# Pairing the leftover attention tiles of neighbouring head pairs, with another order of tiles, normalizations and turns of k and q

## The chip, the cores and the metric

The kernel runs on one NeuronCore of a Trainium2 chip. The metric is the device time of one execution in microseconds (us), the median of five runs. Engines are named as the profile names them: PE (matrix multiply; PEld is its weight load), DVE (vector engine), ACT (activation engine), POOL (GpSimd), SP (the queue from which nearly all DMAs are issued). L12 means line 12 of the kernel.

## The reference

Attention with a threshold on 8 batches of 8 heads (576 positions, head size 64), then a two-layer network with the activation h - tanh(h) on the 4608 x 512 result:

```python
scores = scale * np.matmul(q, k.transpose(0, 1, 3, 2))
thresh = np.max(scores, axis=-1, keepdims=True) - tau
scores = np.where(scores >= thresh, scores, -1000000000.0)
scores = scores - np.max(scores, axis=-1, keepdims=True)
attn = np.exp(scores)
attn = attn / (np.sum(attn, axis=-1, keepdims=True) + 1e-09)
attn_out = np.matmul(attn, v)
...
x = attn_out.transpose(0, 2, 1, 3).reshape(B * S, H * D)   # B*S = 4608, H*D = 512
h = x @ w_in                                               # d_ff = 2048
out = (h - np.tanh(h)) @ w_out
```

## The kernel before

**Tiles.** The 64 heads are taken in 32 pairs p. A head has 576 query rows: four tiles of 128 rows, and 64 rows over. The 64 rows over of the two heads of a pair make one *shared* tile. So a pair has nine tiles (TPP = 9), 288 in all, numbered i = 9p + j. Before the change j = 0 to 3 are the first head, j = 4 is the shared tile, j = 5 to 8 the second head.

**Duos.** The four tiles of a head go in two *duos*: kinds "A" (j = 0, 2, 5, 7) and "B" (the tile after it). A duo's two score tiles are thresholded into one buffer z of 2 x 576 = 1152 columns, which is 9 blocks of 128; it is transposed, exponentiated and multiplied with v together. Where the 9 blocks are cut, the middle block holds the last 64 columns of the A tile beside the first 64 of the B tile; v is therefore kept with two half-empty chunks (4 and 5 of vb), one for each half. The shared tile is alone (kind "M"): its 576 columns stand in a buffer zm with 64 columns of padding, 5 blocks.

**The main loop** goes over steps s from -8 to about 292. One step issues, in this order, for different tiles:

- shift(s+7): the threshold bias nb of a duo (or of an M tile) on DVE, L354
- scores(s+8): PE matmuls of q against k in two fp16 parts, kT and kS, into a psS buffer of the pool ps_big (2 buffers), L327, or L317 for the shared tile; then on DVE the scaled copy with row maximum, L337
- kink(s+5): ACT writes z, L374; after the second tile of a duo (or an M tile) a DMA transpose z to zT on SP's queue, L382. The first six pairs transpose on PE instead (psZ, L394)
- weights(s): ACT's exp of zT into pT, L411 (L403 for the first six pairs)
- the network's work, about one piece in a step: four matmuls 128x512, of psH (L495) or of psY (L521), with tanh on ACT (L508) and h - tanh(h) on DVE (L514), and the copy yo of a finished psY (L534)
- attend(s-2): at the second tile of a duo, ten matmuls of pT and vb into psO (L440); for the shared tile five (L429)
- norm: DVE divides psO by its last column (L454, L455, for the shared rows L460), at j = 4 and j = 8; emit_x of the pair before at j = 1: PE transposes (L472, L478) and two DVE copies (L485, L486)
- what plan holds for this step: DMA loads of k, q and v, the split of k and q in two fp16 parts and of v on POOL (L190 to L194, L222 to L227), and turn

In the first four pairs weights and attend run four steps ahead of these numbers.

**turn(p, "k")** makes pair p's kT: nine PE transposes into a ps_big buffer (L241), a DVE copy (L264), then two POOL copies with the head halves swapped, kS (L270). turn(p, "q") makes qT in the same way without a swap; for odd p from 8 on, and p = 30, it is one DMA transpose instead (L253). Both stand at a distance before first = 9p - 8, the step that issues pair p's first scores: k at first - 5, q at first - 3 (by DMA first - 5). For p = 1 they are nearer.

Each engine works through its instructions in the order in which the loop issued them. The network's 32 pieces for a batch (four pairs, 36 steps) begin at the fifth step of the next batch, and are through when its 36 steps end; so at the first four steps of each batch (s = 36b to 36b + 3) PE has attention work alone. The text calls these four steps the *gap*. After step 292 only the network's last pieces are left (the *tail*).

To speak of places in the new order, r is the number of the step within two pairs: r = s mod 18, from 0 to 17, where the first pair is even.

Of the kernel before, what the change touches and what calls it, by code (L numbers as in the profile page):

```python
# [18 lines left out]
def kernel(  # L19
# [11 lines left out]
    nc = tc.nc  # L31
    P = 128
# [14 lines left out]
    NPAIR = B * HPAIR  # L47
    DM_C = d_model // P
    DF_C = d_ff // P
    TPP = 9  # L50
    NTILE = NPAIR * TPP

# [32 lines left out]
    NV = 4  # L85
    vbs = []
    for i in range(NV):
# [3 lines left out]
        nc.gpsimd.memset(vb[0:64, :, 4, D : D + 1], 1.0)  # L91
        nc.gpsimd.memset(vb[64:P, :, 5, D : D + 1], 1.0)
        vbs.append(vb)

    NM = 2
    zms = []
    for i in range(NM):
        zm = const.tile([P, 5 * P], BF16, name=f"zm{i}")
        nc.vector.memset(zm[:, S : 5 * P], -STEEP)
        zms.append(zm)  # L100

    mx3 = []
# [140 lines left out]
    def q_by_dma(p):  # L245

        return p >= 2 * HPAIR and (p % 2 == 1 or p == 30)
# [48 lines left out]
    REM = (slice(512, 576), slice(576, 640))  # L296
    scs, mxs, nbs, zs, zts, pts, ops = {}, {}, {}, {}, {}, {}, {}

    def kind(j):

        return "M" if j == 4 else "A" if j in (0, 2, 5, 7) else "B"

    def scores(i):
        p, j = divmod(i, TPP)
        qT, kT, kS = mats[p, "q"], mats[p, "k"], mats[p, "ks"]
        ps = ps_big.tile([P, 1024], F32, name="psS", tag="big")
        main, rem, lo = slice(0, 512), slice(512, 576), 0
        if kind(j) == "B":
            main, rem, lo = slice(512, 1024), slice(448, 512), 448
        if j == 4:  # L310
            qrem = REM
            if q_by_dma(p):
                qrem = (slice(512, 640, 2), slice(513, 640, 2))
            for n, kk in enumerate((kT, kS)):
                for dst, srcs in ((main, MAIN), (rem, REM)):
                    for hh in range(2):
                        nc.tensor.matmul(  # L317
                            out=ps[64 * hh : 64 * hh + 64, dst],
                            lhsT=qT[:, qrem[hh]], rhs=kk[:, srcs[hh]],
                            start=(n == 0), stop=(n == 1),  # L320
                        )
        else:
            hh = int(j > 4)
            lhs = qT[:, j * P : (j + 1) * P]
            for n, kk in enumerate((kT, kS)):
                for dst, src in ((main, MAIN[hh]), (rem, REM[hh])):
                    nc.tensor.matmul(  # L327
                        out=ps[:, dst], lhsT=lhs, rhs=kk[:, src],
                        start=(n == 0), stop=(n == 1),
                    )  # L330
        sc = sc_pool.tile([P, S], F32, name="sc")
        if kind(j) == "B":
            mx = mxs[i] = mxs.pop(i - 1)
        else:
            mx = mxs[i] = mx3[i // 2 % len(mx3)]
        c = int(kind(j) == "B")
        nc.vector.tensor_scalar(  # L337
            out=sc, in0=ps[:, lo : lo + S], scalar1=SC, scalar2=None,
            op0=ALU.mult, op1=ALU.max, accum_out=mx[:, c : c + 1],
        )  # L340
        scs[i] = sc

    def shift(i):

        kd = kind(i % TPP)
        if kd == "A":
            return
        mx = mxs.pop(i)
        nb = st_pool.tile([P, 9], F32, name="nb", tag="nb")
        o, m = nb[:, 0:1], mx[:, 0:1]  # L350
        if kd == "B":
            o = nb.rearrange("p (a b) -> p a b", b=3)[:, :, 0:2]
            m = mx.rearrange("p (a b) -> p a b", b=4)[:, :, 0:3]
        nc.vector.tensor_scalar(  # L354
            out=o, in0=m, scalar1=-1.0, scalar2=tau, op0=ALU.mult, op1=ALU.add
        )
        if kd == "B":
            nbs[i - 1], nbs[i] = nb[:, 0:1], nb[:, 1:2]
        else:
            nbs[i] = nb[:, 0:1]  # L360

    def kink(i):
        sc, nb = scs.pop(i), nbs.pop(i)
        kd = kind(i % TPP)
        if kd == "B":
            zt = zs.pop(i - 1)
            z = zt[:, S:W]
        elif kd == "A":
            zt = zs[i] = z_pool.tile([P, W], BF16, name="z")
            z = zt[:, 0:S]  # L370
        else:
            zt = zms[i // TPP % NM]
            z = zt[:, 0:S]
        nc.scalar.activation(  # L374
            out=z, in_=sc, func=ACT.Prelu, bias=nb, scale=1.0, alpha=STEEP
        )
        if on_pe(i):
            zts[i] = zt
        elif kd != "A":
            n = 5 if kd == "M" else TPP  # L380
            zts[i] = zt_pool.tile([P, TPP, P], BF16, name="zT")
            nc.sync.dma_start_transpose(out=zts[i][:, 0:n, :], in_=zt)  # L382

    def weights(i):


        kd = kind(i % TPP)
        n, off = {"A": (4, 0), "M": (5, 0), "B": (5, 4)}[kd]
        if on_pe(i):
            z = zts.pop(i)  # L390
            pl, tag = (ps_h, "h") if i % 2 and i < HPAIR * TPP else (ps_y, "y")
            ps = pl.tile([P, 5 * P], BF16, name="psZ", tag=tag)
            for c in range(n):
                nc.tensor.matmul(  # L394
                    out=ps[:, c * P : (c + 1) * P],
                    lhsT=z[:, (off + c) * P : (off + c + 1) * P],
                    rhs=ident_bf, is_transpose=True, start=True, stop=True,
                )
            if kd == "B":
                pt = pts.pop(i - 1)  # L400
            else:
                pt = p_pool.tile([P, TPP * P], FP16, name="pT")
            nc.scalar.activation(  # L403
                out=pt[:, off * P : (off + n) * P], in_=ps[:, 0 : n * P], func=ACT.Exp
            )
        elif kd == "A":
            return
        else:
            n += off
            pt = p_pool.tile([P, TPP * P], FP16, name="pT")  # L410
            nc.scalar.activation(  # L411
                out=pt[:, 0 : n * P], in_=zts.pop(i)[:, 0:n, :], func=ACT.Exp
            )
        pts[i] = pt

    def attend(i):

        p, j = divmod(i, TPP)
        kd, vb = kind(j), vbs[p % NV]
        if kd == "A":  # L420
            return
        if j in (1, 6):
            ops[p, int(j > 4)] = ps_o.tile([P, 6, D + 1], F32, name="psO", tag="o")
        po = ops[p, int(j > 4)]
        if kd == "M":
            pt = pts.pop(i)

            for c in range(5):
                nc.tensor.matmul(  # L429
                    out=po[:, 4:6, :], lhsT=pt[:, c * P : (c + 1) * P],  # L430
                    rhs=vb[:, :, c, :], start=(c == 0), stop=(c == 4),
                )
            return
        pt, hh = pts.pop(i), int(j > 4)

        for ab in range(2):
            blocks = [(4 * ab + ab + c, c) for c in range(4)]
            blocks.append((4, 4 + ab))
            for n, (blk, c) in enumerate(blocks):
                nc.tensor.matmul(  # L440
                    out=po[:, (j - 1 - 5 * hh) + ab, :],
                    lhsT=pt[:, blk * P : (blk + 1) * P], rhs=vb[:, hh, c, :],
                    start=(n == 0), stop=(n == 4),
                )

    osb = {}

    def norm(p, hh):
        po = ops.pop((p, hh))
        if hh == 0:  # L450
            osb[p] = o_pool.tile([P, 5, 2, D], BF16, name="osb")
        n = 5 - hh
        rc = st_pool.tile([P, 5], F32, name="rc", tag="rc")
        nc.vector.reciprocal(out=rc[:, 0:n], in_=po[:, 0:n, D])  # L454
        nc.vector.tensor_tensor(  # L455
            out=osb[p][:, 0:4, hh, :], in0=po[:, 0:4, 0:D],
            in1=rc[:, 0:4].unsqueeze(2).to_broadcast([P, 4, D]), op=ALU.mult,
        )
        if hh == 0:
            nc.vector.scalar_tensor_tensor(  # L460
                out=osb[p][:, 4, :, :], in0=po[:, 4:6, 0:D], scalar=rc[:, 4:5],
                in1=own, op0=ALU.mult, op1=ALU.mult,
            )
# [191 lines left out]
    for p in range(1, NPAIR):  # L655
        first = TPP * p - AHEAD
        for d, f in PREP[3 if p == 1 else 0 :]:
            d -= p == 1 and d in (3, 5)
            plan.setdefault(first - d, []).append(lambda p=p, f=f: f(p))
        d = 5 if q_by_dma(p) else 3 - (p == 1)  # L660
        plan.setdefault(first - d, []).append(lambda p=p: turn(p, "q"))

    load(0, "v")
# [27 lines left out]
    for s in range(-AHEAD, NTILE + LAG + 3):  # L691
# [37 lines left out]
        for i in atts.pop(s, []):  # L729
            pp, jj = divmod(i, TPP)  # L730
            if i < NTILE:
                attend(i)
            if i < NTILE and jj in (4, 8):
                norm(pp, int(jj > 4))
            if jj == 1 and pp:
                emit_x(pp - 1)
        for step in plan.pop(s, []):
            step()
# [61 lines left out]
```

## Time and profile before

| | |
|---|---|
| median of five runs | 537.08 us (536.77 to 538.00) |
| the profiled execution | 537.77 us, its span from first to last instruction 536.0 us |
| granted PE clock | 0.999 of full speed |
| DVE score copies (L337) | 288 of 752 ns |
| ACT z (L374), exp of a duo from zT (L411) and of a shared tile | 768 ns, 1154 ns and 726 ns |
| ACT exp from psZ (L403), 640 and 512 columns | 706 and 599 ns |
| DVE nb (L354), of a duo and of a shared tile | 155 and 144 ns |
| DMA transposes of z, of zm, of q | 104, 26 and 13; 3.5, 2.7 and 3.3 us to landing |

How to read it: "busy" of PE counts matmuls whose ends are modelled, and the mean of a matmul row is its latency, several times what it adds to a dense stream. What a group of matmuls costs is therefore read from the timeline, as the time from its first start to the start of the next group. A time in brackets on a timeline line is idle time of the engine before it, with the instruction that ended it.

### The profile page before, as it was taken

The page shows a single profiled execution, that of the slowest core. Times are in us where ns is not written, and L with a number is a line of the kernel's source. Part 1 is how long each engine was busy: PE and PEld are TensorE (multiplying, and loading weights), DVE is VectorE, ACT ScalarE, POOL GpSimd, SP SyncE. Part 2 cuts the span into 40 slices and gives each one's busy share as a digit, 9 for nine tenths or more (in the row PEclk, how much of TensorE's full clock was granted, in tenths as well). Part 3 has the DMA queues.
Part 4 walks back from the last instruction along what each step waited for, and adds up shares of the span by engine and source line. Part 5 has one row for each costly group of instructions (what it writes and reads, how often), then busy time and mean ns, then how long its engine had stood idle before and what let it go on. Part 6 is the DMA issues. An engine that isn't in the chain of part 4 may idle for free.

```text
span 536.0 us, 13042 instructions
## 1 busy us (share of the span) xinstructions
PE 513.6 (96%) x4782; PEld 288.0 (54%) x4782; DVE 427.5 (80%) x1202; ACT 438.2 (82%) x630; POOL 291.0 (54%) x390
## 2 busy tenths in 40 slices
PE   8989899999999999999999999999999999999997
PEld 3666565555555555555555555555555455444444
DVE  5889888988888988889888988898888888554440
ACT  5999888999898989899888989898989989543330
POOL 7999996767555666657555755566665720000000
PEclk9999999999999999999999999999999999999999
DMA  6654648989997999799988999899989885401113
GB/s 197 189 182 149 207 144 156 208 172 180 173 191 176 166 206 189 169 184 190 189 187 183 189 185 184 169 179 193 191 162 186 188 152 112 105 21 39 39 41 78
DMA packets 204768, 85.76 MB, mean 160 GB/s; under 512 B 172320, under 2 KB 197152, under 8 KB 204704
## 3 DMA queue, kind: packets, MB, share of 16 engines
q1 hardware_dynamic: 204112, 84.51, 74.7%
q8 instruction: 37, 0.61, 0.5%
q10 hardware_dynamic: 592, 0.43, 0.3%
q14 instruction: 27, 0.22, 0.1%
HBM read 36.70 MB, written 9.44 MB: 86 GB/s over the span
## 4 chain that ended last, share of the span: by engine, by line
PE 67%; DVE 16%; POOL 7%; ACT 3%; issue 3%; DMA 2%; SPq 0%; DVEq 0%; POOLq 0%; ACTq 0%
PE psY L521 21%; PE psH L495 17%; PE psS L327 14%; DVE sc L337 7%; PE psO L440 5%; DVE g L514 3%; PE psS L317 3%; PE psHt L495 3%; PE ps_k L241 2%; DVE kT L264 2%; DMA qT<-qhl 2%; ACT pT L403 2%; POOL kS L270 1%; ACT z L374 1%; DVE yo L534 1%
## 5 line engine op out<-in xcount | busy, mean ns | idle before, releaser
L337 DVE TENSOR_SCALAR_CACHE_REDUCE sc<-psS 128x576 f32<-128x576 f32 x288 | 216.1, 752 | 23.1 <-PE psS L327 14.1
L374 ACT ACTIVATE z<-sc,nb 128x576 bf16<-128x576 f32 x256 | 193.4, 768 | 19.6 <-DVE nb L354 19.4
L521 PE MATMUL psY<-w_out_sb,g 128*128 128x512 bf16 (+1 forms) x592 | 146.0, 374 | 0.8 <-DVE yo L534 0.8
L411 ACT ACTIVATE pT<-zT 128x1152 f16<-128x1152 bf16 (+1 forms) x130 | 138.9, 1068 | 0.9 <-DMA zT<-z 0.9
L270 POOL COPY kS<-kT 64x1152 f16<-64x1152 f16 x62 | 70.9, 1143 | 126.2 <-DVE nb L354 124.6
L495 PE MATMUL psH<-xT,w_in_sb 128*128 128x512 bf16 x480 | 124.0, 379 | 2.3 <-DVE g L514 2.3
L327 PE MATMUL psS<-kT,qT 128*128 128x512 f16 (+1 forms) x512 | 104.4, 285 | 6.7 <-DVE sc L337 3.7
L508 ACT ACTIVATE th<-psH 128x512 f32<-128x512 f32 x128 | 75.5, 590 | 36.7 <-PE psH L495 35.6
L327 PEld LDWEIGHTS <-qT 128*128 128x128 f16 x1024 | 72.4, 97 | 56.8 <-issue 9.0
L327 PE MATMUL psS<-kS,qT 128*128 128x512 f16 x496 | 101.3, 286 | 0.8 <-POOL kS L270 0.7
L514 DVE SCALAR_TENSOR_TENSOR g<-th,psH 128x512 bf16<-128x512 f32 x128 | 87.3, 682 | 17.8 <-ACT th L508 17.8
L521 PEld LDWEIGHTS <-g 128*128 128x128 bf16 x592 | 50.7, 98 | 56.8 <-issue 4.0
L495 PEld LDWEIGHTS <-w_in_sb 128*128 128x128 bf16 x576 | 49.2, 98 | 58.2 <-issue 4.5
L440 PEld LDWEIGHTS <-pT 128*128 128x128 f16 x1280 | 55.7, 98 | 25.2 <-issue 1.9
L440 PE MATMUL psO<-vb,pT 128*128 128x65 bf16 x1280 | 61.2, 193 | 0.0
L194 POOL TENSOR_TENSOR khl<-kraw,khl 128x576 f16<-128x576 f32 x31 | 39.7, 1281 | 2.6
L194 POOL TENSOR_TENSOR qhl<-qraw,qhl 128x576 f16<-128x576 f32 x31 | 39.7, 1281 | 2.6
L403 ACT ACTIVATE pT<-psZ 128x640 f16<-128x640 bf16 (+1 forms) x54 | 35.5, 658 | 5.8 <-PE psZ L394 5.6
L264 DVE COPY kT<-ps_k 128x1152 f16<-128x1152 f16 x31 | 23.4, 756 | 14.1 <-PE ps_k L241 14.0
L534 DVE COPY yo<-psY 128x512 f32<-128x512 f32 (+1 forms) x31 | 21.1, 682 | 13.1 <-PE psY L521 11.1
L455 DVE TENSOR_TENSOR osb<-psO,rc 128x256 bf16<-128x256 f32 x64 | 27.2, 425 | 2.2
L354 DVE TENSOR_SCALAR nb<-mx 128x6 f32<-128x6 f32 (+1 forms) x160 | 24.5, 153 | 2.3
(81 smaller groups left out, 509.5 us busy)
## 6 DMA issues: line engine op xcount, KB each, us to landing
vraw<-in_v_dram SPq DMA_DIRECT2D x32, 256.0 KB, 3.6
out_dram<-yo SPq DMA_DIRECT2D x32, 256.0 KB, 2.9
kraw<-in_k_dram SPq DMA_DIRECT2D x31, 256.0 KB, 3.6
qraw<-in_q_dram SPq DMA_DIRECT2D x31, 256.0 KB, 3.8
wt<-in_moe_w_in_dram SPq DMA_DIRECT2D x8, 512.0 KB, 4.7
wt<-in_moe_w_out_dram SPq DMA_DIRECT2D x8, 512.0 KB, 4.2
zT<-z SPq DMA_TRANSPOSE x104, 3.5
kraw<-in_k_dram SPq DMA_DIRECT2D x32, 32.0 KB, 3.3
```

The lines of the kernel that those rows point to most:

```text
L194: nc.gpsimd.tensor_tensor(out=hl[:, :, 1, :], in0=x, in1=hl[:, :, 0, :], op=ALU.subtract)
L270: nc.gpsimd.tensor_copy(out=o, in_=i)
L327: nc.tensor.matmul(out=ps[:, dst], lhsT=lhs, rhs=kk[:, src], start=(n == 0), stop=(n == 1),)
L337: nc.vector.tensor_scalar(out=sc, in0=ps[:, lo : lo + S], scalar1=SC, scalar2=None, op0=ALU.mult, op1=ALU.max, accum_out=mx[:, c : c + 1],)
L374: nc.scalar.activation(out=z, in_=sc, func=ACT.Prelu, bias=nb, scale=1.0, alpha=STEEP)
L403: nc.scalar.activation(out=pt[:, off * P : (off + n) * P], in_=ps[:, 0 : n * P], func=ACT.Exp)
L411: nc.scalar.activation(out=pt[:, 0 : n * P], in_=zts.pop(i)[:, 0:n, :], func=ACT.Exp)
L440: nc.tensor.matmul(out=po[:, (j - 1 - 5 * hh) + ab, :], lhsT=pt[:, blk * P : (blk + 1) * P], rhs=vb[:, hh, c, :], start=(n == 0), stop=(n ...
L495: nc.tensor.matmul(out=ps, lhsT=w_in_sb[:, c, n * P : (n + 1) * P], rhs=xs[m][:, c, :] if m < B else xR[:, c, :, :], start=(c == 0), stop= ...
L508: nc.scalar.activation(out=th, in_=ps, func=ACT.Tanh)
L514: nc.vector.scalar_tensor_tensor(out=gs[m][:, n, :], in0=th, scalar=-1.0, in1=ps, op0=ALU.mult, op1=ALU.add,)
L521: nc.tensor.matmul(out=ps, lhsT=gs[m][:, n, ms * P : (ms + 1) * P], rhs=w_out_sb[:, n, cols], start=(n == 0), stop=(n == DF_C - 1),)
```

## The change

The nine tiles of a pair are put in another order. In an even pair the shared tile goes last (j = 8), in an odd pair first (j = 0), so that the shared tiles of two neighbours stand beside each other and form a duo of their own; A and B now simply alternate (kind(i) is "AB"[i % 2]). The kind M, with its buffers zm, is gone: 160 shifts become 144, and 130 DMA transposes of z become 117 (all of 9 blocks).

attend takes the middle block of a duo once for both tiles, a matmul with 130 columns of vb in place of two with 65: nine matmuls in place of ten. A shared duo is multiplied in two halves, five matmuls each: that of the even pair at once, that of the odd pair two steps later, with that pair's first duo, which opens its psO. The shared rows of an even pair are now normalized with its second head, of an odd pair with its first.

The normalizations now fall at r = 5 and 11 for the even pair and r = 15 and 1 for the odd one (11 and 15 with the shared rows), emit_x at r = 3 and 13. From p = 5 on, k is turned at first - 3 for even p (r = 7) and at first - 6 for odd p (r = 13); q at first - 2 (r = 8 for even p), by DMA still at first - 5.

```diff
-    NM = 2
-    zms = []
...
-    def kind(j):
-        return "M" if j == 4 else "A" if j in (0, 2, 5, 7) else "B"
+    def kind(i):
+        return "AB"[i % 2]
+
+    def place(i):
+        p, j = divmod(i, TPP)
+        j = j - p % 2
+        return (p, None, 4) if j in (-1, 8) else (p, j // 4, j % 4)
...
     def scores(i):
-        p, j = divmod(i, TPP)
+        p, hh, t = place(i)
...
-            hh = int(j > 4)
-            lhs = qT[:, j * P : (j + 1) * P]
+            lhs = qT[:, (5 * hh + t) * P : (5 * hh + t + 1) * P]
...
     def attend(i):
-        p, j = divmod(i, TPP)
-        kd, vb = kind(j), vbs[p % NV]
-        if kd == "A":
+        if kind(i) == "A":
             return
-        if j in (1, 6):
-            ops[p, int(j > 4)] = ps_o.tile([P, 6, D + 1], F32, name="psO", tag="o")
...
-        for ab in range(2):
-            blocks = [(4 * ab + ab + c, c) for c in range(4)]
-            blocks.append((4, 4 + ab))
-            for n, (blk, c) in enumerate(blocks):
-                nc.tensor.matmul(
-                    out=po[:, (j - 1 - 5 * hh) + ab, :],
-                    lhsT=pt[:, blk * P : (blk + 1) * P], rhs=vb[:, hh, c, :],
-                    start=(n == 0), stop=(n == 4),
-                )
+        p, hh, t = place(i)
+        vb, pt = vbs[p % NV], pts[i]
+        if hh is None:
+            attend_shared(p - 1, 0, pt)
+            return
+        if t == 1:
+            ops[p, hh] = ps_o.tile([P, 6, D + 1], F32, name="psO", tag="o")
+            if p % 2 and hh == 0:
+                attend_shared(p, 1, pts.pop(i - 2))
+        po = ops[p, hh]
+        nc.tensor.matmul(
+            out=po[:, t - 1 : t + 1, :], lhsT=pt[:, 4 * P : 5 * P],
+            rhs=vb[:, hh, 4:6, :], start=True, stop=False, skip_group_check=True,
+        )
+        for n in range(8):
+            ab, c = divmod(n, 4)
+            blk = 5 * ab + c
+            nc.tensor.matmul(
+                out=po[:, t - 1 + ab, :], lhsT=pt[:, blk * P : (blk + 1) * P],
+                rhs=vb[:, hh, c, :], start=False, stop=(n == 7), skip_group_check=True,
+            )
+        pts.pop(i)
+
+    def attend_shared(p, ab, pt):
+        vb = vbs[p % NV]
+        for n in range(5):
+            blk, c = ((5 * ab + n, n) if n < 4 else (4, 4 + ab))
+            nc.tensor.matmul(
+                out=ops[p, 1 - p % 2][:, 4:6, :], lhsT=pt[:, blk * P : (blk + 1) * P],
+                rhs=vb[:, :, c, :], start=(n == 0), stop=(n == 4),
+            )
...
     def norm(p, hh):
-        n = 5 - hh
+        shared = hh != p % 2
+        n = 4 + shared
...
             d -= p == 1 and d in (3, 5)
+            if d == 5 and p >= 5:
+                d = 6 if p % 2 else 3
             plan.setdefault(first - d, []).append(lambda p=p, f=f: f(p))
-        d = 5 if q_by_dma(p) else 3 - (p == 1)
+        d = 5 if q_by_dma(p) else (2) if p >= 5 else 3 - (p == 1)
...
-            if i < NTILE and jj in (4, 8):
-                norm(pp, int(jj > 4))
-            if jj == 1 and pp:
+                odd = pp % 2
+                if jj == 3 + odd:
+                    norm(pp, 0)
+                elif odd and jj in (0, 8):
+                    norm(pp - (jj == 0), 1)
+            if pp and jj == 1 + pp % 2:
                 emit_x(pp - 1)
```

More of the change, by code (lines that the diff above doesn't have):

```diff
@@ L93 @@
         vbs.append(vb)
-    NM = 2
-    zms = []
[L97 to L100, printed above, removed]
     mx3 = []
@@ L307, in scores @@
         main, rem, lo = slice(0, 512), slice(512, 576), 0
-        if kind(j) == "B":
+        if kind(i) == "B":
             main, rem, lo = slice(512, 1024), slice(448, 512), 448
-        if j == 4:
+        if hh is None:
             qrem = REM
@@ L331, in scores @@
         sc = sc_pool.tile([P, S], F32, name="sc")
-        if kind(j) == "B":
+        if kind(i) == "B":
             mx = mxs[i] = mxs.pop(i - 1)
@@ L335, in scores @@
             mx = mxs[i] = mx3[i // 2 % len(mx3)]
-        c = int(kind(j) == "B")
+        c = int(kind(i) == "B")
         nc.vector.tensor_scalar(
@@ L343, in shift @@
     def shift(i):
-        kd = kind(i % TPP)
-        if kd == "A":
+        if kind(i) == "A":
             return
@@ L349, in shift @@
         nb = st_pool.tile([P, 9], F32, name="nb", tag="nb")
[L350 to L353, printed above, removed]
         nc.vector.tensor_scalar(
-            out=o, in0=m, scalar1=-1.0, scalar2=tau, op0=ALU.mult, op1=ALU.add
-        )
[L357 to L360, printed above, removed]
+            out=nb.rearrange("p (a b) -> p a b", b=3)[:, :, 0:2],
+            in0=mx.rearrange("p (a b) -> p a b", b=4)[:, :, 0:3],
+            scalar1=-1.0, scalar2=tau, op0=ALU.mult, op1=ALU.add,
+        )
+        nbs[i - 1], nbs[i] = nb[:, 0:1], nb[:, 1:2]
     def kink(i):
         sc, nb = scs.pop(i), nbs.pop(i)
-        kd = kind(i % TPP)
-        if kd == "B":
+        if kind(i) == "B":
             zt = zs.pop(i - 1)
             z = zt[:, S:W]
-        elif kd == "A":
+        else:
             zt = zs[i] = z_pool.tile([P, W], BF16, name="z")
-            z = zt[:, 0:S]
-        else:
-            zt = zms[i // TPP % NM]
             z = zt[:, 0:S]
@@ L378, in kink @@
             zts[i] = zt
-        elif kd != "A":
-            n = 5 if kd == "M" else TPP
+        elif kind(i) == "B":
             zts[i] = zt_pool.tile([P, TPP, P], BF16, name="zT")
-            nc.sync.dma_start_transpose(out=zts[i][:, 0:n, :], in_=zt)
+            nc.sync.dma_start_transpose(out=zts[i], in_=zt)
     def weights(i):
-        kd = kind(i % TPP)
-        n, off = {"A": (4, 0), "M": (5, 0), "B": (5, 4)}[kd]
+        kd = kind(i)
+        n, off = {"A": (4, 0), "B": (5, 4)}[kd]
         if on_pe(i):
@@ L416, in attend @@
     def attend(i):
-        p, j = divmod(i, TPP)
-        kd, vb = kind(j), vbs[p % NV]
-        if kd == "A":
+        if kind(i) == "A":
             return
-        if j in (1, 6):
-            ops[p, int(j > 4)] = ps_o.tile([P, 6, D + 1], F32, name="psO", tag="o")
[L424 to L431, printed above, removed]
-                )
-            return
-        pt, hh = pts.pop(i), int(j > 4)
-        for ab in range(2):
-            blocks = [(4 * ab + ab + c, c) for c in range(4)]
-            blocks.append((4, 4 + ab))
-            for n, (blk, c) in enumerate(blocks):
-                nc.tensor.matmul(
-                    out=po[:, (j - 1 - 5 * hh) + ab, :],
-                    lhsT=pt[:, blk * P : (blk + 1) * P], rhs=vb[:, hh, c, :],
-                    start=(n == 0), stop=(n == 4),
-                )
+        p, hh, t = place(i)
+        vb, pt = vbs[p % NV], pts[i]
+        if hh is None:
+            attend_shared(p - 1, 0, pt)
+            return
+        if t == 1:
[23 more added lines that the diff above has]
+            )
     osb = {}
@@ L458, in norm @@
         )
-        if hh == 0:
+        if shared:
             nc.vector.scalar_tensor_tensor(
```

## The prediction, made before the changed kernel was run

> **What bounds the kernel now.** First the page's chain that ended last: it is PE for two thirds. Then busy time by stretches, since such a sum hides stages.
>
> ```profile
> PE 67%; DVE 16%; POOL 7%; ACT 3%; issue 3%; DMA 2%; SPq 0%; DVEq 0%; POOLq 0%; ACTq 0%
> 13.00:70.00 57.00, 50.87 (x686) 35.37 (x685) 50.04 (x155) 52.99 (x86) 54.04 (x67) 1.00 0.59 184
> 242.00:300.00 58.00, 57.32 (x544) 31.90 (x542) 51.31 (x147) 52.32 (x73) 34.57 (x45) 1.00 0.94 184
> 470.00:536.00 66.00, 62.27 (x304) 29.49 (x302) 25.33 (x38) 21.84 (x37) 0.00 (x0) 0.99 0.15 44
> ```
>
> Columns: length, then busy PE, PEld, DVE, ACT, POOL. To 70 us, POOL (54 of 57) and ACT (53) bound; from about 126 to 460 us PE is filled (57.3 of 58), DVE and ACT near 90%; the tail is PE alone, and the change doesn't touch it. So in the six middle batches only PE's own work or PE's stalls are worth anything. I took those from the timeline, from start to start.
>
> ```profile
> 256.65 0.59 PE L521 MATMUL psY<-w_out_sb,g 128*128 128x512 bf16 x2
> 257.18 0.44 PE L317 MATMUL psS<-kT,qT 128*64 128x512 f16 x4
> 257.44 0.42 PE L317 MATMUL psS<-kS,qT 128*64 128x512 f16 x4
> 257.79 1.04 PE L495 MATMUL psH<-xT,w_in_sb 128*128 128x512 bf16 x4
> ...
> 260.84 0.46 PE L429 MATMUL psO<-vb,pT 128*128 128x130 bf16 x5
> 261.13 0.41 PE L327 MATMUL psS<-kT,qT 128*128 128x512 f16 x2
> 261.37 0.41 PE L327 MATMUL psS<-kS,qT 128*128 128x512 f16 x2
> 261.62 1.03 PE L495 MATMUL psH<-xT,w_in_sb 128*128 128x512 bf16 x4
> ...
> 266.85 0.47 PE L440 MATMUL psO<-vb,pT 128*128 128x65 bf16 x10
> 267.17 0.41 PE L327 MATMUL psS<-kT,qT 128*128 128x512 f16 x2
> ```
>
> Read off: usual scores 261.13 to 261.62 = 0.49; shared scores 257.18 to 257.79 = 0.61, and two matmuls of L521 (0.22 each by the cadence of this stage, four in 0.86) would have ended at 257.08, so another 0.10 is lost ahead of them: 0.22 more than a usual tile. A duo's attend costs 0.315 (31.5 ns a matmul), a shared tile's 0.29 (58 ns for 130 columns). A network piece is 0.87, a turn on PE 0.50.
>
> Then the stalls. In a batch of 58 us they sum to about 2 us, half of it in the gap:
>
> ```profile
> 237.58 0.48 PE L440 MATMUL psO<-vb,pT 128*128 128x65 bf16 x10
> ...
> 238.20 0.41 PE L327 MATMUL psS<-kT,qT 128*128 128x512 f16 x2
> ...
> 238.26 0.75 DVE L337 TENSOR_SCALAR_CACHE_REDUCE sc<-psS 128x576 f32<-128x576 f32 x1
> ...
> 239.07 0.41 PE L327 MATMUL psS<-kT,qT 128*128 128x512 f16 x2 [0.22 <-DVE sc L337]
> ```
>
> Attend should pass in 0.315 and took 0.62; the scores at 238.20 should have given way at 238.69, not 239.07. PE waits for a psS buffer while DVE copies without pause: 0.31 + 0.38, and 0.16 after that, 0.85 us in each gap.
>
> Last, the way of a k turn to kS:
>
> ```profile
> 158.25 0.67 PE L241 MATMUL ps_k<-ident_f,khl 128*128 128x128 f16 x9
> ...
> 159.02 0.76 DVE L264 COPY kT<-ps_k 128x1152 f16<-128x1152 f16 x1 [0.49 <-PE ps_k L241]
> ...
> 159.91 2.33 POOL L270 COPY kS<-kT 64x1152 f16<-64x1152 f16 x2 [6.21 <-DVE nb L354]
> ```
>
> The copy starts 0.77 after the turn, kS is done at 162.24, 3.99 after it. Of the turns later than 110 us most show 0.77, those soon after a gap 1.09, one 1.47.
>
> **What the skill says.** "TensorE: Matmul & The Clock Gate", section "Wait — 56ns, not 53.3ns?": a warm matmul costs its columns at 2.4 GHz and a fixed 2.5 ns. So merging two of 65 into one of 130 saves the fixed part alone; the trace agrees in kind (63 against 58 ns). The same page, section "What happens when you issue a matmul": only weight loads are pulled ahead, matmuls stay in order; so a wait on kS holds all that PE has behind it. "SBUF — State Buffer", section "SBUF: two separate sides": DVE and POOL share a port pair, by which kS could be held up; in this trace its 62 copies lie between 1140 and 1146 ns, so I add nothing.
>
> **Part by part.**
>
> *Attend*: 10 x 31.5 = 315 ns becomes 58 + 8 x 31.5 = 310. 5 ns x 128 duos = 0.64 us, of which the PE-bound part has four fifths: **-0.5**.
>
> *Shared scores into the gap.* Scores run 8 steps ahead, so tiles 8 and 9 of every four pairs are issued at the gap's first two steps, tiles 26 and 27 among network work as before. Two shared tiles leave the filled stretch, 0.22 each, and lengthen a stretch where PE waits 0.85 anyway: 0.44 x 6 gaps = **-2.6** (bounds 0, if DVE's chain is pushed by them, and -3.5 if a stall beside them goes as well). Late next is DVE's copying, which stays.
>
> *Shifts, exps, transposes.* 16 nb fewer (16 x 144 ns = 2.3 us of DVE), 13 x (2 x 726 - 1154) = 3.9 us of ACT, 13 DMA issues of about 1.26 us on SP: hidden behind PE in the middle, **0**. In the first six pairs, near ACT's limit: an exp pair of 2 x 706 becomes 706 + 599, three times, **-0.3**; three PE transposes fewer at 0.055, -0.2 (together **-0.5**). Buffers: a shared pT is kept two steps longer, but is free two steps ahead of the third duo after it, so no wait is added.
>
> *k of even pairs, first - 3.* From the turn to the first need of kS PE issues: turn 0.50; scores 0.49, piece 0.87, q turn 0.50; scores 0.49, piece 0.87, attend 0.31; kT half 0.25: 4.28 us, against 3.99 for kS, or 4.31 where DVE starts at 1.09. Behind this wait stand all of PE's next scores and pieces. POOL has split v just before, 1.2 us, and reaches kS idle. Pairs 10 to 28: on the edge, 0 to 0.2 each, taken as **+0.6** in all. Pair 30 turns q by DMA, so PE has 3.78: **+0.2**. Pairs 6 and 8 stand where the network fills only part of the steps; k turns at 71.07 and 101.23 us, 18 steps apart, make a step there 1.68: 2 x 1.68 + 0.75 = 4.1, late by little if DVE is prompt and by 0.3 each at a start of 1.1: **+0.3** (0 to 1.0).
>
> *k of odd pairs, first - 6.* Only p = 5 hurts: its k part left POOL, which has no pause there, at 58.31 and the turn began at 58.37; one step earlier PE waits up to 1.2. ACT has z work meanwhile: **+0.6** (0 to 1.3). Later k shares a step with emit_x (DVE 0.63 + 0.76), but q and the normalization are away: 0.
>
> *q turns, first - 2.* Before, k, the long normalization and q followed in three steps; now two steps have the turns alone. The stalls behind q of pair 6 (0.56 at 74.4 us) and of pair 8 (0.47 at 105) should shrink: **-0.8** (-1.0 to +0.5). Pair 30's q transpose was issued 3.9 us after its k turn, queued on SP behind a zT and a store, and PE lost 1.04 on it; in the new order that step has no zT: **-0.5** (-1.0 to 0).
>
> Sum: -0.5 - 2.6 - 0.5 + 0.6 + 0.2 + 0.3 + 0.6 - 0.8 - 0.5 = -3.2. The profiled execution took 537.77 (span 536.0 and 1.8 around it), 0.7 over the median of 537.08; so 534.6 for that execution, **533.9** as a median.
>
> **Rivals.** *More is freed* (chance 0.16): all of a batch's 1.7 us of stalls that are not jitter go, gap, yo and issue, and the early waits don't come: 6 x 1.3 = 8, about 529. For it: the turns no longer meet a normalization. Against: DVE is at 88% whatever the order, and the gap is DVE's. *Nothing comes of it* (0.10): the gap's DVE chain is pushed by the shared tiles, the early waits eat the rest: 536.6. *Slower* (0.24): kS comes late in all 13 even pairs from 6 to 30, because DVE reaches the kT copy late. Lateness is the copy's start + 3.22 - 4.28; the other terms sum to -4.3, so it decides from 0.33 each, a start 1.39 after the turn. At 1.7, late by 0.64: 13 x 0.64 - 4.3 = +4, 541. For it: 1.09 and 1.47 occur, and the cover is two steps, before four. Against: most starts are at 0.77, and nothing heavy stands on DVE at r = 6 and 7.
>
> **How the numbers follow.** The forecast has 0.50, spread by its unknown terms from about 531.5 to 536. Five runs of this kernel differ by 0.2%, so I call within 0.2% (536.0 to 538.2) the same. Faster 0.66, same 0.10, slower 0.24. The range goes from 529.5, near the fast rival, to 538.8, the mild half of the slow one.
>
> **What would show it.** Right: the gap's stalls at a batch's start fall from 0.85 to about 0.5 and a middle batch from 58.0 to 57.4; kS waits on PE under 0.2; a wait of k's turn for khl near 57 us. Wrong: PE waits for POOL's kS of over 0.3 in each even pair, or batches still of 58 us.

## The result, and the profile after

The changed kernel takes 535.58 us (median of 22 runs, 533.76 to 537.45), the kernel before 537.41 in the runs beside it (43 runs): ratio 0.9965 [0.9958, 0.9973], or 1.9 us less. The execution that was profiled took 537.45, the slowest of the 22, with a span of 535.7; its trace shows too little of the gain and, as will be seen, why. In what follows lines of code are those of the changed kernel: L326 and L317 are the usual and the shared scores, L336 their copy by DVE, L420 and L427 attend (merged block and the other eight), L438 the shared attend, L235 the turn on PE, L258 its copy to kT or qT, L264 kS, L247 q's DMA, L370 the zT DMA, L519 and L493 network pieces.

First the page after: busy times, then the chain that ended last.

```profile
PE 510.6 (95%) x4651; PEld 289.3 (54%) x4651; DVE 423.7 (79%) x1184; ACT 436.8 (82%) x617; POOL 290.1 (54%) x390
...
PE 59%; DVE 10%; POOL 9%; DMA 8%; ACT 8%; issue 5%; SPq 0%; ACTq 0%; POOLq 0%; DVEq 0%
PE psY L519 19%; PE psH L493 15%; PE psS L326 13%; DMA qT<-qhl 5%; ACT z L363 3%; PE psO L427 3%; PE psHt L493 3%; DVE sc L336 3%; DVE g L512 2%; POOL kS L264 2%; PE psS L317 2%; DVE yo L532 2%; ACT pT L399 2%; ACT th L506 2%; DMA zT<-z 2%
```

PE has 3 us less to do (513.6 before). DVE's part of the chain fell from 16 to 10%; but DMA went from 2 to 8%, and 5% of the chain is now q's transpose. The windows of the middle say the same (length; busy PE, PEld, DVE, ACT, POOL; clock, DMA share, GB/s):

```profile
242.00:300.00 58.00, 56.90 (x528) 32.17 (x527) 50.97 (x146) 51.93 (x71) 34.47 (x45) 1.00 0.97 181
300.00:358.00 58.00, 57.43 (x531) 32.38 (x530) 51.50 (x146) 52.61 (x72) 34.19 (x45) 1.00 0.89 183
```

Two stretches of the same work: one keeps PE busy as before, the other leaves it idle for half a us more. The waits of PE name the cause. Kernel before first (engine and line, what it waited for; us in total, times, longest):

```profile
PE psS L327 <- DVE sc L337: 3.7, 13, 0.8
...
PE ps_q L241 <- POOL qhl L194: 1.9, 4, 1.0
...
PE psS L327 <- DMA qT<-qhl: 1.1, 2, 0.9
```

And after:

```profile
PE psS L317 <- DMA qT<-qhl: 3.7, 5, 0.9
...
PE psS L326 <- DMA qT<-qhl: 1.0, 1, 1.0
...
PE psS L326 <- DVE sc L336: 0.7, 3, 0.4
...
PE ps_q L235 <- POOL qhl L188: 0.8, 1, 0.8
...
PE ps_k L235 <- POOL khl L188: 0.6, 2, 0.5
...
PE psS L317 <- POOL kS L264: 0.4, 1, 0.4
```

The wait of scores for DVE's score copies, at which the order aimed, fell from 3.7 to 0.7 (0.8 more now stands ahead of two turns, which use the same buffers). The wait for kS that the slower rival needed thirteen times didn't come: the one of 0.4 us stands at 18.9 us, ahead of all moved turns, and the kernel before has it too, 0.4 at 18.6. In their place PE waits six times for q's DMA: 4.7 us, against 1.1 before.

One gap with q in time, PE's timeline (start, duration):

```profile
351.46 1.03 PE L519 MATMUL psY<-w_out_sb,g 128*128 128x512 bf16 x4
352.32 0.22 PE L420 MATMUL psO<-vb,pT 128*128 128x130 bf16 x1
352.38 0.42 PE L427 MATMUL psO<-vb,pT 128*128 128x65 bf16 x8
352.73 0.44 PE L317 MATMUL psS<-kT,qT 128*64 128x512 f16 x4
...
353.24 0.42 PE L317 MATMUL psS<-kT,qT 128*64 128x512 f16 x4
...
353.84 0.23 PE L420 MATMUL psO<-vb,pT 128*128 128x130 bf16 x1
...
354.27 0.41 PE L326 MATMUL psS<-kT,qT 128*128 128x512 f16 x2
...
354.95 0.41 PE L326 MATMUL psS<-kT,qT 128*128 128x512 f16 x2
...
355.74 0.23 PE L420 MATMUL psO<-vb,pT 128*128 128x130 bf16 x1
...
356.81 1.03 PE L493 MATMUL psH<-xT,w_in_sb 128*128 128x512 bf16 x4
```

From the last network piece to the next: 356.81 - 351.46 = 5.35 us. Before it was 5.36 to 5.39 in every gap, with no shared tile in it; now two are, and it is no longer. The stalls left: 0.12 in the second attend (0.43 for 0.31), 0.19 ahead of the scores at 354.95 (0.68 for 0.49), 0.30 ahead of the attend at 355.74: 0.61, where there were 0.85.

Three of the six gaps of the same trace are longer: one of 6.22 (from 117.75), two of 6.05 (235.32 to 241.37 and 293.24 to 299.29). In the first of these two, on the same engine:

```profile
236.85 0.42 PE L317 MATMUL psS<-kS,qT 128*64 128x512 f16 x4
238.04 0.44 PE L317 MATMUL psS<-kT,qT 128*64 128x512 f16 x4 [0.77 <-DMA qT<-qhl]
```

The bracket is idle time and its releaser: the second shared tile is the first to read the odd pair's q, which had not landed. The same outside a gap, with SP's queue beside PE:

```profile
198.98 0.54 SPq L535 DMA_DIRECT2D out_dram<-yo  x1
199.61 0.38 SPq L145 DMA_DIRECT2D qraw<-in_q_dram  x1
200.05 0.55 SPq L153 DMA_DIRECT2D qraw<-in_q_dram  x1
200.69 1.94 SPq L370 DMA_TRANSPOSE zT<-z  x1
...
202.73 1.31 SPq L247 DMA_TRANSPOSE qT<-qhl  x1
...
207.78 0.39 PEld L317 LDWEIGHTS <-qT 128*64 128x64 f16 x8 [1.21 <-DMA qT<-qhl]
207.78 0.44 PE L317 MATMUL psS<-kT,qT 128*64 128x512 f16 x4 [0.71 <-DMA qT<-qhl]
```

Each DMA starts within 0.1 us of the end of the one ahead: q's transpose doesn't wait for data, it waits its turn behind a store, two loads and a zT that took 1.94 us to issue. Issued at 202.73, it lands at about 207.75, 5.0 us later; PE wanted it at 207.07. The weight load of q idles longer (1.21) than the matmuls (0.71), as the Trainium skill has it in "TensorE: Matmul & The Clock Gate", section "What happens when you issue a matmul": only weight loads are pulled ahead; this trace agrees, the load stands idle 0.5 us sooner than the matmuls. The matmuls' figure is the loss.

Read in this way for the ten odd pairs that want their q between 140 and 415 us, the time from issue to need has a median of 4.8 us before (4.0 to 5.5) and 4.2 after (2.8 to 4.7). The landing (the time from issue until the data is there), from the view of the DMA's line, is no shorter. Before:

```profile
DMA to landing us min/median/max: 3.3/3.3/5.5
```

After:

```profile
DMA to landing us min/median/max: 3.3/4.0/5.1
```

So 0.6 us of slack (the time from issue to need) went from a transfer that lands anywhere between 3.3 and 5.5 us. Two experiments below divide it. As means of the ten the slack is 4.8 us before and 4.0 after; it is 4.4 in the new order with all the old turns (oldturns), and 4.4 in the changed kernel with the odd pairs' k at its old place (oddk5). About half went with the new order and half with k's turn, whose 0.50 us on PE had stood between issue and need. What in the order takes its half was not separated.

### The profile page after: what moved, and what is told of

It is laid out like the page before. It is cut to its first block, busy times and chain, and to the rows that moved or that the text cites. A ratio compares the mean times of both kernels' runs of the same rounds, so it can differ in the third digit from the quotient of the medians.

```text
span 535.7 us, 12822 instructions
## 1 busy us (share of the span) xinstructions
PE 510.6 (95%) x4651; PEld 289.3 (54%) x4651; DVE 423.7 (79%) x1184; ACT 436.8 (82%) x617; POOL 290.1 (54%) x390
## 4 chain that ended last, share of the span: by engine, by line
PE 59%; DVE 10%; POOL 9%; DMA 8%; ACT 8%; issue 5%; SPq 0%; ACTq 0%; POOLq 0%; DVEq 0%
PE psY L519 19%; PE psH L493 15%; PE psS L326 13%; DMA qT<-qhl 5%; ACT z L363 3%; PE psO L427 3%; PE psHt L493 3%; DVE sc L336 3%; DVE g L512 2%; POOL kS L264 2%; PE psS L317 2%; DVE yo L532 2%; ACT pT L399 2%; ACT th L506 2%; DMA zT<-z 2%
## 5 line engine op out<-in xcount | busy, mean ns | idle before, releaser
L336 DVE TENSOR_SCALAR_CACHE_REDUCE sc<-psS 128x576 f32<-128x576 f32 x288 | 214.5, 753 | 40.2 <-PE psS L326 22.3
L363 ACT ACTIVATE z<-sc,nb 128x576 bf16<-128x576 f32 x288 | 217.0, 769 | 31.8 <-DVE nb L348 29.6
L519 PE MATMUL psY<-w_out_sb,g 128*128 128x512 bf16 (+1 forms) x592 | 145.9, 373 | 0.8 <-DVE yo L532 0.8
L264 POOL COPY kS<-kT 64x1152 f16<-64x1152 f16 x62 | 70.9, 1144 | 126.8 <-DVE nb L348 125.2
L399 ACT ACTIVATE pT<-zT 128x1152 f16<-128x1152 bf16 x117 | 135.0, 1153 | 3.0 <-DMA zT<-z 1.2
L493 PE MATMUL psH<-xT,w_in_sb 128*128 128x512 bf16 x480 | 123.3, 379 | 2.3 <-DVE g L512 2.3
L326 PE MATMUL psS<-kT,qT 128*128 128x512 f16 (+1 forms) x512 | 104.4, 285 | 4.8 <-DVE qT L258 1.2
L326 PEld LDWEIGHTS <-qT 128*128 128x128 f16 x1024 | 74.3, 97 | 59.7 <-issue 5.4
L326 PE MATMUL psS<-kS,qT 128*128 128x512 f16 x496 | 101.4, 286 | 0.0
L519 PEld LDWEIGHTS <-g 128*128 128x128 bf16 x592 | 51.0, 98 | 56.8 <-issue 2.4
L493 PEld LDWEIGHTS <-w_in_sb 128*128 128x128 bf16 x576 | 49.1, 98 | 57.0 <-issue 4.7
L427 PE MATMUL psO<-vb,pT 128*128 128x65 bf16 x1024 | 53.3, 194 | 0.0
L427 PEld LDWEIGHTS <-pT 128*128 128x128 f16 x1024 | 44.2, 98 | 9.5
L391 ACT ACTIVATE pT<-psZ 128x512 f16<-128x512 bf16 (+1 forms) x54 | 35.0, 652 | 5.0 <-PE psZ L382 4.6
L420 PE MATMUL psO<-vb,pT 128*128 128x130 bf16 x128 | 28.2, 220 | 0.4
L258 DVE COPY kT<-ps_k 128x1152 f16<-128x1152 f16 x31 | 23.3, 752 | 5.8 <-PE ps_k L235 5.8
```

The lines of the kernel that those rows point to most:

```text
L264: nc.gpsimd.tensor_copy(out=o, in_=i)
L326: nc.tensor.matmul(out=ps[:, dst], lhsT=lhs, rhs=kk[:, src], start=(n == 0), stop=(n == 1),)
L336: nc.vector.tensor_scalar(out=sc, in0=ps[:, lo : lo + S], scalar1=SC, scalar2=None, op0=ALU.mult, op1=ALU.max, accum_out=mx[:, c : c + 1],)
L363: nc.scalar.activation(out=z, in_=sc, func=ACT.Prelu, bias=nb, scale=1.0, alpha=STEEP)
L391: nc.scalar.activation(out=pt[:, off * P : (off + n) * P], in_=ps[:, 0 : n * P], func=ACT.Exp)
L399: nc.scalar.activation(out=pt[:, 0 : n * P], in_=zts.pop(i)[:, 0:n, :], func=ACT.Exp)
```

## The experiments

Every ratio is to the kernel before, in the runs beside it.

**q's DMA one step earlier, in the changed kernel (q6).**

```
-        d = 5 if q_by_dma(p) else (2) if p >= 5 else 3 - (p == 1)
+        d = 6 if q_by_dma(p) else (2) if p >= 5 else 3 - (p == 1)
```

> The changed kernel with one edit: q's DMA transpose is issued at first - 6 in place of first - 5. Theory of the cover: in the changed kernel's profile PE waits 4.7 us for qT (mostly the shared tile of an odd pair), because k's turn (0.50 on PE) has left the five steps between the DMA's issue and its first use, while the DMA stands on SP behind a zT and takes 3.3 to 5.1 us to land. Then one step more (1.6 us) takes these waits away: under 1 us in all, and the time falls by 1.5 to 3.5 us against the changed kernel, ratio to the kernel before 0.990 to 0.994. Rival, the DMA engines are full and the transpose lands late wherever it is issued: waits of over 3 us remain and the ratio stays at 0.9965.

532.97 us, ratio 0.9921 [0.9907, 0.9936], and no wait for q's DMA is left on PE. The same place of the timeline:

```profile
197.29 0.67 PE L235 MATMUL ps_k<-ident_f,khl 128*128 128x128 f16 x9
197.32 0.54 SPq L535 DMA_DIRECT2D out_dram<-yo  x1
...
197.96 1.52 SPq L247 DMA_TRANSPOSE qT<-qhl  x1
...
199.54 0.77 SPq L145 DMA_DIRECT2D qraw<-in_q_dram  x1
200.36 0.56 SPq L153 DMA_DIRECT2D qraw<-in_q_dram  x1
...
201.02 1.28 SPq L370 DMA_TRANSPOSE zT<-z  x1
...
205.50 0.44 PE L317 MATMUL psS<-kT,qT 128*64 128x512 f16 x4
```

q now stands ahead of the loads and of zT, 7.5 us before its need (205.50 - 197.96). Its landing, median 3.8 and up to 5.8, is hardly another, so it is the earlier issue that took the waits away. The changed kernel loses 0.44% here, about 2.4 us. Its 22 runs spread over 3.7 us, 43 of the kernel before over 2.6, the six of q6 over 1.4: that fits a landing of 3.3 to 5.1 us, needed after 4.2, though six runs show less of a spread than 22 in any case.

**Two steps earlier (q7).** The same line with `d = 7`.

> The changed kernel with q's DMA transpose at first - 7. With one step earlier (first - 6) PE did not wait for qT at all any more, so if the wait was the whole of it a second step brings nothing: ratio 0.991 to 0.9935. Rival, q at first - 7 stands ahead of POOL's split of q, SP waits for POOL and the zT behind it come late: ratio 0.995 or more, ACT waiting for zT.

533.76 us, 0.9934 [0.9918, 0.995]. Nothing more is seen; one step is enough.

**One step earlier in the kernel before (q6_before).**

```
-        d = 5 if q_by_dma(p) else 3 - (p == 1)
+        d = 6 if q_by_dma(p) else 3 - (p == 1)
```

> The kernel before with q's DMA transpose issued at first - 6 in place of first - 5. Theory of the cover: here k's turn still lies between the DMA and its first use, and PE waits for qT only for 1.4 us at two places (pair 23 or 25, and pair 30), so it gains 0.5 to 1.5 us, ratio 0.997 to 0.999, much less than the 2.4 that the same edit brought to the changed kernel. Rival, an earlier q is worth the same in both: ratio 0.9955 or less.

536.12 us, 0.998 [0.9972, 0.9987]: 1.1 us, as much as the trace of before showed of this wait. So q was late before too, and the change about doubled what that costs: 2.4 less 1.1 is 1.3 us, to which the intervals of the two leave about 1 us either way.

**The new order with all the old turns (oldturns).**

```
-            if d == 5 and p >= 5:
-                d = 6 if p % 2 else 3
...
-        d = 5 if q_by_dma(p) else (2) if p >= 5 else 3 - (p == 1)
+        d = 5 if q_by_dma(p) else 3 - (p == 1)
```

> The new order of tiles with all turns as before the change (k at first - 5, q at first - 3, by DMA first - 5). By the prediction's terms the moved turns cost 1.1 (kS, k of pair 5) and bring 0.8, so old turns leave the time near the changed kernel, and the regained cover of q's DMA takes 0.5 to 2 us off: ratio 0.993 to 0.997. Rival, the turns have to stand between the normalizations: k and the shorter normalization share r = 5, q and nothing at r = 7, k at 14 beside the long one at 15; PE then waits for DVE and the ratio is 0.999 to 1.003.

539.53 us, 1.0042 [1.0027, 1.0057], above both of the ranges expected: the new order without the moved turns makes the kernel slower. The timeline of this run shows where an even pair's turn now stands:

```profile
302.28 0.69 DVE L532 COPY yo<-psY 128x512 f32<-128x512 f32 x1
...
302.39 0.66 PE L235 MATMUL ps_k<-ident_f,khl 128*128 128x128 f16 x9
...
302.89 0.68 DVE L512 SCALAR_TENSOR_TENSOR g<-th,psH 128x512 bf16<-128x512 f32 x1
...
303.48 0.18 DVE L452 RECIPROCAL rc<-psO 128x4 f32<-128x4 f32 x1
...
303.69 0.43 DVE L453 TENSOR_TENSOR osb<-psO,rc 128x256 bf16<-128x256 f32 x1
...
304.03 0.75 DVE L258 COPY kT<-ps_k 128x1152 f16<-128x1152 f16 x1
...
304.83 0.41 PE L326 MATMUL psS<-kT,qT 128*128 128x512 f16 x2 [0.42 <-DVE kT L258]
```

The turn meets a normalization on DVE, with yo and g ahead of it; its own copy starts 1.64 after the turn instead of 0.77, and ps_k keeps one of the buffers that scores also use. At the second score tile after the turn PE waits 0.42 for that buffer. So it goes in every second even pair from 10 to 30 (starts of 1.64 to 1.74; pair 8, at 1.73, has no yo and was late before). In the pairs between, 12 to 28, g and the normalization stand ahead of the copy too, but no yo, and it starts at 0.86 us. So it takes both to make it late. This run's waits count it:

```profile
PE psS L326 <- DVE kT L258: 3.6, 9, 0.5
```

In the new order the moved turns are thus worth 0.77% (1.0042 - 0.9965), 4.1 us.

**The old turns with q's DMA early (oldq6).** The edit of oldturns, with `d = 6` for q's DMA.

> The new order with all turns of k and of q on PE as before the change, q by DMA at first - 6. The new order with old turns lost 0.42%; its profile has 2.4 us of PE waiting for qT, 3.6 for kT's copy and 1.6 for q's. If the late DMA is the main part of that loss: ratio 0.996 to 0.9995. If it is the collision of turns and normalizations (DVE copies late, psS buffers not free): it stays, ratio 1.0005 to 1.003.

539.39 us, 1.0033 [1.002, 1.0046], a little above the range for the collision of turns and normalizations. The difference to oldturns, 0.09%, lies inside the intervals: q's DMA is a small part of that loss at most. With q in time on both sides (this run against q6) the moved turns are worth 1.12%, 6.0 us.

**Only the even pairs' turns old (evenold).**

```
-                d = 6 if p % 2 else 3
+                d = 6 if p % 2 else 5
...
-        d = 5 if q_by_dma(p) else (2) if p >= 5 else 3 - (p == 1)
+        d = 5 if q_by_dma(p) else (2) if p >= 5 and p % 2 else 3 - (p == 1)
```

> The changed kernel with the even pairs' turns as before the change (k at first - 5, q at first - 3), the odd ones as changed. By the prediction's terms for even pairs (kS late +1.1, q's stalls -0.8) within 0.5 us of the changed kernel, ratio 0.9955 to 0.9975, with the q stalls of pairs 6 and 8 back (0.5 each) and kS never late. Rival, the even turns' new place between r = 5 and r = 11 carries the gain: ratio 0.999 or more, DVE idle less and PE waiting for psS buffers about r = 5 to 7.

537.02 us, 1.0000 [0.999, 1.001], with `PE psS L326 <- DVE kT L258` at 4.9 us in 10 waits. The even pairs' turns bring 0.35%.

**Only the odd pairs' k old (oddk5), and that with q's DMA early (oddk5q6).**

```
-                d = 6 if p % 2 else 3
+                d = 5 if p % 2 else 3
```

> The changed kernel with k of odd pairs turned at first - 5 again (even pairs as in the change). Theory of the cover: k's turn is back between q's DMA and its use, so the waits for qT fall from 4.7 us to under 2.5 and the time by 0.5 to 2 us, ratio 0.993 to 0.9955; it also shares steps with nothing heavy but the normalization at r = 15. Rival, the place of k among the normalizations is what matters: DVE work bunches at r = 14 and 15, PE waits for DVE's copies, ratio 0.998 or more.

536.30 us, 0.9985 [0.9978, 0.9993].

> The changed kernel with q by DMA at first - 6 and k of odd pairs at first - 5, beside the long normalization at r = 15. With q on time in both, the difference from q alone (0.9921) is the place of k. If the collision with the normalization costs 0.3 us in each of 13 odd pairs: ratio 0.998 to 1.000. If the odd place is indifferent and only q's lateness counted: 0.9905 to 0.9935.

536.65 us, 0.9985 [0.9978, 0.9991]. Together with the changed kernel and q6 this makes a square:

| | q's DMA at first - 5 | at first - 6 |
|---|---|---|
| odd k at first - 5 | 0.9985 (oddk5) | 0.9985 (oddk5q6) |
| odd k at first - 6 | 0.9965 (after) | 0.9921 (q6) |

An earlier q is worth 0.44% with k early, and nothing with k late; the early k is worth 0.64% where q is in time, 0.20% where it isn't. The two waits stand in for one another: k's removal gives PE time that q's DMA takes back. To see it inside single executions, I read from PE's timeline the start of `psX<-fold` in emit_x at every fourth pair from 140 us on; the differences are the lengths of four batches:

| kernel | lengths of four successive batches, us |
|---|---|
| before | 58.17, 57.96, 57.96, 57.96 |
| after | 57.70, 58.71, 58.22, 57.42 |
| q6 | 57.44, 57.43, 57.43, 57.43 |
| oddk5 | 58.03, 58.02, 58.03, 58.04 |
| oldq6 | 58.48, 58.49, 58.49, 58.84 |

Where q is in time, a batch of the changed kernel is 57.42, that of q6; each late q adds 0.5 to 0.8 (the 0.27 of the first batch isn't one). Odd k at first - 5 costs 0.6 in each batch. Of this 0.23 stands in the gap (5.58 us in oddk5q6, against 5.35), where attend waits for its exp (timeline of oddk5q6):

```profile
238.47 0.23 PE L420 MATMUL psO<-vb,pT 128*128 128x130 bf16 x1 [0.38 <-ACT pT L399]
```

Ahead of it DVE has the kT copy and the long normalization one after the other; that score copies, and with them z and the exp, come late by this is likely and was not tried apart. The rest is a pause of 0.16 us at the odd pair by the gap and of 0.20 at the other, ahead of the network piece that follows emit_x. The list of waits doesn't show it, the timeline does:

```profile
255.83 0.68 DVE L512 SCALAR_TENSOR_TENSOR g<-th,psH 128x512 bf16<-128x512 f32 x1
...
256.12 0.41 PE L326 MATMUL psS<-kS,qT 128*128 128x512 f16 x2
...
256.56 1.02 PE L493 MATMUL psH<-xT,w_in_sb 128*128 128x512 bf16 x4
```

The piece should follow the scores after 0.25, at 256.37; it starts 0.05 after the end of DVE's g, which reads the psH that the piece will write. In q6 k's turn stands ahead of the same piece on PE, and it starts 0.36 to 0.40 after g with no pause. So k's earlier place hides a wait for g in every odd pair.

**What PE's work costs in the gap and outside it (gapmm, offmm).** In the kernel before, one matmul of 128 x 512 more in the scores of two tiles of each batch, from i = 72 on, 12 in all; its result is overwritten by the one behind it. In gapmm the tiles are those scored in the gap, in offmm two among network work (`(26, 27)` in the place of `(8, 9)`).

```
+            if i >= 72 and i % 36 in (8, 9):
+                nc.tensor.matmul(
+                    out=ps[:, main], lhsT=lhs, rhs=kT[:, MAIN[hh]], start=True, stop=True,
+                )
```

> The kernel before with one 128x512 matmul (0.22 us, its result is overwritten) added to the scores of tiles 8 and 9 of every four pairs from tile 72 on, 12 in all, 2.6 us of PE work, which PE meets at the first two steps of the gap. If PE has spare time there, as the prediction holds for the shared tiles: no change, ratio 0.999 to 1.001, and the stalls of the gap shrink by 0.4. Rival, DVE's chain in the gap is pushed by it: up to 2.6 us more, ratio 1.004 to 1.005.

> The same 12 matmuls on tiles 26 and 27, 18 steps from the gap, amid network work, where the shared tiles of the other two pairs lie in the new order. If PE is the bound there: 2.6 us more, ratio 1.004 to 1.0055. Rival, PE has spare time there too: ratio under 1.002, and then shared tiles moved to the gap could not have brought 2.6 us.

gapmm: 537.94 us, 1.0012 [1.0003, 1.0022], a little above the range expected. offmm: 539.04 us, 1.0036 [1.0023, 1.0049], a little below. Read as above, a batch is 58.08 in gapmm and 58.40 in offmm against 57.96: of two matmuls, 0.44 us, 0.12 shows in the gap and 0.44 outside. So work of PE is three quarters hidden in the gap and costs its full time elsewhere, which is what the term for the shared scores stood on.

**The merged block of attend alone (attend_b).** In the kernel before, the two 65-column matmuls of a duo's middle block as one of 130:

```
+        nc.tensor.matmul(
+            out=po[:, t : t + 2, :], lhsT=pt[:, 4 * P : 5 * P],
+            rhs=vb[:, hh, 4:6, :], start=True, stop=False, skip_group_check=True,
+        )
+        for n in range(8):
```

> The kernel before with the merged middle block alone: attend takes nine matmuls in place of ten, in the old order of tiles. The prediction's term: 5 ns a duo, 0.5 us in all, ratio 0.9985 to 0.9995; the ten-matmul group of 0.315 us becomes 0.31. Rival, the weight load that goes with the tenth matmul is worth more (0.05 us a duo): 6 us, ratio 0.988 to 0.991.

535.97 us, 0.9978 [0.9968, 0.9989], more than the range expected. Its batches are 57.92 against 57.96, 0.04 for 16 duos: over the whole kernel some 0.3 us. Between its trace and that of before 0.9 us more stands in one batch (57.86 against 58.75), where before waits longer for q's DMA, 0.4 at pair 27 and 0.5 at pair 30. That is a matter of when a transfer lands, and no price of the edit. That the 1.2 of the medians has the same cause isn't shown; no run has this edit with q in time.

**Pair 5's k where it was (q6p5).** q6 with `if d == 5 and p >= 6:`.

> The changed kernel with q by DMA at first - 6 and, besides, k of pair 5 at first - 5 as before the change. The prediction holds that the earlier k of pair 5 costs 0.6 (0 to 1.3), PE waiting for POOL's khl: ratio 0.9895 to 0.9925, the wait of 0.5 for khl gone. Rival, POOL sets that stage's pace and the wait only moves to q or kS: the same as with q alone, 0.992 to 0.9935.

533.10 us, 0.9916 [0.99, 0.9931]: inside the range of the prediction's term, but these intervals don't tell it from q6. The traces say more. PE is 0.8 us ahead of q6 at step 36 and has lost all of it by step 90; at pair 9, about 125 us, it waits 0.4 for ACT's exp, which q6 does not. With q6 it is the fastest version of the study, 0.8% below the kernel before and 0.5% below the changed one.

## Why the prediction was right, and where it was not

The sign, the kind of gain and the losing rival came out as forecast; the size, -3.2, came out at -1.9. Most of that difference is q's DMA; other terms missed too, in both directions.

- *Shared scores into the gap and attend.* For a batch the forecast is 0.44 and 16 x 0.005 = 0.08, -0.52; measured with q in time 57.96 - 57.43 = -0.53. The gap kept its length with two more tiles in it, its stalls went from 0.85 to 0.61 (about 0.5 was forecast). Attend's own part is half of its price, 0.04 a batch. gapmm shows that hidden work isn't quite free, a quarter shows.
- *kS of even pairs, +1.1 in three terms.* Too dear: no even pair from 6 on waits for kS in the trace of after, and in q6 pair 30 alone does, 0.3 (0.2 was forecast for it). With this the slower rival fell. Its point of decision, a copy that starts 1.39 after the turn, is passed once (pair 10, 1.44), with no wait for kS of over 0.15 us; the other even pairs start at 0.77 to 1.31. In oldturns seven of them start at 1.64 to 1.74, but with a cover of four steps in place of two, and what PE waits for there is the buffer of ps_k, not kS.
- *First six pairs, -0.5, and k of pair 5, +0.6.* From the first scores to those of pair 6, at 78 us, five traces of the old order take 70.0 to 70.2 us, after and q6 70.7, q6p5 70.2. So k of pair 5 costs its 0.5 there, and the rest brings nothing. The saving of q6p5 doesn't last to the end.
- *q turns, -0.8, and kS of pairs 6 and 8, +0.3.* Their sum is about right. From pair 6's first scores to the gap at 118 us (tile 79) the trace of before takes 40.1 us, oldturns 38.9, after 38.2: the moved turns bring 0.7 there. The other 1.2 comes with the order alone, and no term had it; before waits there 0.8 for a score copy and 1.0 for g ahead of emit_x, of which after has 0.2. (The fall of the wait for qhl from 1.9 to 0.8 is another matter: those four waits are at q turns of pairs 2 to 5, others took their place, and up to 70 us PE's waits of over 0.15 us rose from 7.8 to 9.7.)
- *The turns were priced against the kernel before alone.* Against the new order with the old turns they are worth 4.1 us (oldturns), because that order moves normalizations onto the old places, and where a copy yo stands there too DVE comes late to kT; no term asked that.
- *"Later k shares a step with emit_x ..., but q and the normalization are away: 0", and pair 30's q at -0.5.* These failed. The order and k's new place together uncovered the DMA of q: the mean slack of an odd pair's q fell from 4.8 us to 4.4 and then to 4.0, while its landing varies between 3.3 and 5.5. PE's waits for it are 1.1 us in the trace of before, 2.4 in oldturns, 4.7 in after. It costs 2.4 us after (q6) and 1.1 before (q6_before), 1.3 more. Pair 30 still loses 0.96: its slack grew from 2.8 to 3.2, and its landing from 3.6 to 4.1. I had looked at the queue for pair 30 alone, though twelve odd pairs turn q in the same way.
- *The sum.* With q in time on both sides the change brings 536.12 - 532.97 = 3.15 us less; the forecast for that is -2.7, its -3.2 without pair 30's -0.5. Add the 1.3 for q and it is -1.9; that this is the measured value is no test, since both parts come from the same four medians. That the total comes so near is partly luck, as terms missed in opposite directions. By the starts of scores in the traces of q6_before and q6:

| stretch | forecast, us | measured, us |
|---|---|---|
| to pair 6's first scores, 78 us | -0.5 + 0.6 = +0.1 | +0.5 |
| to pair 9's, 120 us | +0.3 - 0.8 = -0.5 | -1.8 |
| to pair 29's, 411 us | -2.6 - 0.5 + 0.6 = -2.5 | -2.45 |
| from there to the end | +0.2 | +0.5 |

- *What would show it.* Right: gap's stalls, batch of 57.4 where q lands in time, k's wait for khl (0.5 at 58.6 us). "Batches still of 58" happened too, in two of four, by a cause that wasn't on the list.

One question is settled in part: oddk5 in its trace loses 2.1 us to q's DMA and gains nothing when that is gone. By the starts of scores oddk5q6 wins 0.7 at pair 9 and gives it back at once, as PE then waits 0.5 for an exp; of the 0.4 at pair 21 it wins 0.06, since its gap has a wait for an exp instead; at pair 30 it wins 1.1, of which 0.7 is left six tiles later. Where the rest goes, behind the last scores, isn't settled, nor what in the new order takes its half of q's slack.

## What to carry to other kernels

When an edit takes a stall off the bounding engine, list each transfer that ends in the same stretch with its slack, from issue to need, and set that against the longest landing in the trace and not the median: the one whose slack is inside the spread is the next wait. Issuing such a DMA one step earlier on a full queue cost nothing here and brought more than the change itself (2.4 us against 1.9). And price a reordering against the new order without its companion moves, since half of a change may only repair what the other half breaks.

## What the runs showed of the hardware

- The same transpose of 128 x 1152 two-byte elements lands 3.3 to 5.8 us after its issue within one execution (q6). Its issue keeps SP for 1.3 to 2.8 us (after), and on the queue that is shown the next transfer starts only within 0.1 us behind it, so that neighbours are held up by as much.
- A long landing in one place, not work, can be most of what parts two executions: 0.9 us of the lead of attend_b's trace over that of before stands at two DMAs of q.
